# An attention and MoE kernel on one core: three VectorE operations in the weight conversion, new due times, and transposes in early gaps

## The chip, the cores and the metric

The kernel runs on one core of a Trainium2 chip. The metric is the device time of one execution in microseconds (us), the median of the runs shown. The engines are TensorE (PE, with weight loads listed apart as PEld), VectorE (DVE), ScalarE (ACT), GpSimd (POOL) and SyncE (SP, which here only issues DMAs). Each engine works through its own queue in order; they wait for each other through semaphores.

## What is computed

A linear attention over 8 batches, 8 heads, 576 positions and 64 columns feeds a two-layer network with a squared rectifier. The inputs lie in DRAM as 32-bit floats, apart from the two weight matrices, which are 64-bit floats; the output is 32-bit.

```
q_s = softmax of q over the columns of a head
k_s = softmax of k over the positions
kv  = k_s^T v                 per batch and head
x   = q_s kv                  laid out as 4608 tokens x 512
h   = x @ w_in                512 -> 2048
g   = s * max(h, 0)^2 + b
out = g @ w_out               2048 -> 512
```

## The kernel before

Matmuls run on fp32r values. To keep precision each weight, each `x` and each `g` is split into a high and a low part, and each product is three matmuls (high x high, high x low, low x high), 128 x 128 by 128 x 512.

The 4608 tokens are nine blocks: eight of 512 tokens, one for each batch (positions 0 to 511), and a last one made of the 64 positions left over of each batch. The hidden width of 2048 is cut into 16 pieces of 128, so a block has 16 steps. A step `t` (function `step`) is: 12 matmuls `h<-x,w` (line 975), then the rectifier on ACT (`r`, line 1000), squaring, scale and bias, the split into `gh` and `gl`, and 12 matmuls into `acc` (line 1038). In the even steps of the first block and in all later ones the middle goes DVE (line 1013), ACT (1015), DVE (1017). In the odd steps of the first block it goes ACT (1004), ACT (1006), ACT (1008), DVE (1010).

**Weights.** Weights arrive in 16 chunks `f` of 1 MB: `w_in` and `w_out` parts of one hidden piece, fetched on SP's queue by `load_w` into a staging tile `st`, where the low word `lo` and the high word `hi` of each 64-bit weight lie side by side. `conv_w` turns a chunk into 32-bit floats with integer and float operations on the two words, and splits it. Before the change it does this, each line one instruction on 1024 elements a partition (chunk 0 in two halves):

- ACT, line 204: `low` = `lo` scaled by 2^-29, as an integer
- ACT, line 207: `lo` = absolute value of `hi`, as floats
- DVE, line 210: the two top bits of `low` = those of `hi`, its sign among them
- DVE, line 215: clamp `lo` between C_MIN and C_MAX
- DVE, line 217: mask `lo` and shift it left by 3
- DVE, line 220: `low` = `lo` + `low`; from here the staging tile is free for a later chunk
- ACT, line 225: `w` high = `low` rounded to fp32r
- DVE, line 227: `w` low = `low` - `w` high

Chunk `f` is needed by step `f` of the first block (its `w_in` half by `h`, its `w_out` half by `acc`). So all 16 conversions stand beside the first block, as does the attention of batch 1. The attention of batch 0 stands before it. That attention is, for a pair of heads `u`, `k_stream` (maximum, `early` = exp, transposes, copies), `kv_stream` (`kv` matmuls and the blocks `kvf`), and `q_stream` (maximum, subtraction, exp, sum, division, transpose `qT`, copy to `early` in line 437, matmuls `xp` in line 444, cast to `x` in line 450, low part in line 453). The first step can end only when all four `x` of batch 0 are there.

**What sets the order.** Each piece of work is a generator that yields `Op`s: engine, an assumed cost, a due time, what it needs, which buffers it takes and frees. `Order.run` walks a model of the engines: among the operations of one engine that could start within 0.1 us of the earliest, it takes the one with the lowest due time, and then emits its instructions. The order on every queue, SP's and POOL's among them, is fixed by that when the program is built. Due times are in steps: `DUE_K`, `DUE_Q` and `DUE_V` have an entry for each pair of heads (batch 0 first, then batch 1) or each group of two pairs, and a conversion of chunk `f` is due at `f - AHEAD`, the first at `DUE_W`. A due time orders only operations that compete; it delays nothing by itself.

**Gaps on PE.** When the model sees PE without work for some time, it calls `idle`, which issues transposes of the identity into a PSUM bank that is not in use yet (`unused`, the bank tagged `h`), 60% of the gap at 0.109 us each. This ends when the first step takes the bank.

**Buffers.** PSUM: `acc` two, `big`, `sm` and `h` one each. SBUF: three `tmp` (the `low` of a conversion takes one), 17 `w` (staging tiles and finished weights).

Of the kernel before, what the change touches and what calls it, by code (L numbers as in the profile page):

```python
# [8 lines left out]
F32 = mybir.dt.float32  # L9
F32R = mybir.dt.float32r  # L10
I32 = mybir.dt.int32
U32 = mybir.dt.uint32
U16 = mybir.dt.uint16
AF = mybir.ActivationFunctionType
ALU = mybir.AluOpType
AX = mybir.AxisListType


C_MIN = 2.0 ** -15
C_MAX = float.fromhex("0x1.dffffep+16")  # L20

# [3 lines left out]
def attention_moe(ctx: ExitStack, tc: tile.TileContext, q, k, v, w_in, w_out, s, b, out):  # L27
    nc = tc.nc
# [3 lines left out]
    P = 128  # L32
# [5 lines left out]
    TB = NQ * P  # L38
    NTMP = 3
    NFE = 5  # L40
    AHEAD = 1
    PACE = 6

    DUE_K = (-42.5, 0, -33.5, -16, 6.5, 14, 12.5, 8.5)
    DUE_Q = (-8.5, -4.5, -2, -1, 13.5, 9.5, -29, 88.5)
    DUE_V = (-80, -87.5, -7.5, 14)
    DUE_W = -8
    assert DM == H * D and DM == NP * P and 2 * D == P and 2 * LEFT == P and B * LEFT == TB

    const = ctx.enter_context(tc.tile_pool(name="const", bufs=1))  # L50
# [6 lines left out]
    ps = ctx.enter_context(tc.tile_pool(name="ps", bufs=1, space=bass.MemoryType.PSUM))  # L57


    ident = const.tile([P, P], F32, name="ident")  # L60
# [57 lines left out]
    class Order:  # L118
# [28 lines left out]
        def run(self, streams):  # L147
            heads = [[next(g), 0.0, g] for g in streams]
            while heads:
                can = [(self.start(o, ready), i) for i, (o, ready, g) in enumerate(heads)]  # L150
                can = [(t, i) for t, i in can if t is not None]
                first, i = min(can)
                eng = heads[i][0].eng
                t, i = min(
                    ((t, i) for t, i in can if heads[i][0].eng == eng and t <= first + self.NEAR),
                    key=lambda c: (heads[c[1]][0].due, c),
                )
                o, ready, g = heads[i]
                if eng == "PE":

                    self.idle(t - self.at[eng], "h" in o.take)

                heads[i][1] = end = self.at[eng] = t + o.cost * (2 if eng == "PE" and t < self.COLD else 1)
                if o.kb:
                    self.pipe = max(self.pipe, end) + o.kb / 1024 / self.RATE
                    end = self.pipe + self.TRIP
                for tag in o.take:
                    self.taken[tag] += 1
                for tag in o.free:
                    self.freed[tag].append(end + self.HOP)  # L170
                for n in o.gives:
                    self.done[n] = end, "DMA" if o.kb else eng
                heads[i][0] = after = next(g, None)
                if after is None:
                    del heads[i]
                elif not o.kb and (eng != "PE" or after.eng != eng):
                    heads[i][1] = end + self.HOP
# [14 lines left out]

    def conv_w(f, some):

        due = f - AHEAD if f else DUE_W
        n = some.stop - some.start
        two = n / 2
        last = some.stop == 2
        yield Op("ACT", 1.04 * two, due, needs=[f"w{f} {i} there" for i in range(some.start, some.stop)], take=["tmp"])
        stg = wst[f][:, some]  # L200
        lo, hi = stg[:, :, :, 0], stg[:, :, :, 1]
        low = work.tile([P, n, DO], U32, name=f"low{some.start}_{f}", tag="tmp", bufs=NTMP)

        nc.scalar.activation(low.bitcast(I32), lo, AF.Copy, scale=2.0 ** -29)
        yield Op("ACT", 1.04 * two, due)

        nc.scalar.activation(lo.bitcast(F32), hi.bitcast(F32), AF.Abs)  # L207
        yield Op("DVE", 0.6 * two, due)

        nc.vector.tensor_scalar(  # L210
            low.bitcast(U16).rearrange("p n (e t) -> p n e t", t=2)[:, :, :, 1], stg.bitcast(U16)[:, :, :, 3],
            0xC000, None, op0=ALU.bitwise_and
        )
        yield Op("DVE", 0.6 * two, due)
        nc.vector.tensor_scalar(lo.bitcast(F32), lo.bitcast(F32), C_MIN, C_MAX, op0=ALU.max, op1=ALU.min)
        yield Op("DVE", 0.6 * two, due)
        nc.vector.tensor_scalar(lo, lo, 0x07FFFFFF, 3, op0=ALU.bitwise_and, op1=ALU.logical_shift_left)
        yield Op("DVE", 1.13 * two, due, free=["w"] if last else (), gives=[f"w{f} {some.stop} read"])

        nc.vector.tensor_tensor(out=low, in0=lo, in1=low, op=ALU.add)  # L220
        yield Op("ACT", 0.98 * two, due, take=["w"] if some.start == 0 else ())
        if not wt[f]:
            wt[f] = wpool.tile([P, 2, 2, DO], F32R, name=f"w_{f}", tag="w")
        w = wt[f][:, some]
        nc.scalar.copy(w[:, :, 0], low.bitcast(F32))
        yield Op("DVE", 1.13 * two, due, free=["tmp"], gives=[f"w{f} {i}" for i in range(some.start, some.stop)])
        nc.vector.tensor_tensor(out=w[:, :, 1], in0=low.bitcast(F32), in1=w[:, :, 0].bitcast(F32), op=ALU.subtract)
        for i in range(n):
            if some.start + i == 0:
                wi[f] = w[:, i].rearrange("p t (c e) -> p t c e", c=NP)  # L230
            else:
                wo[f] = w[:, i]
# [93 lines left out]
    def k_stream(u):  # L326
        pr, i = divmod(u, 2)
        due, (tag, bufs) = DUE_K[u], wide(u)
        yield Op("PE", 0.6, due, needs=[f"k{u} there"], take=["big", "ke"])
# [22 lines left out]
    def k_pair(pr):  # L352
        us = (2 * pr, 2 * pr + 1)
        due = DUE_K[us[0]]

# [24 lines left out]
    def kv_second(pr):  # L380
        due = DUE_V[pr]
        yield Op("PE", 1.4, due, needs=[f"k{u}" for u in (2 * pr, 2 * pr + 1)] + [f"v{pr} there"], take=["sm"], gives=[f"kv{pr}"])
# [8 lines left out]
    def kv_stream(pr):  # L391
        us = (2 * pr, 2 * pr + 1)
        due = DUE_V[pr]
        yield Op("DVE", 0.33, due, needs=[f"z{u}" for u in us])
# [9 lines left out]
    def q_stream(u):  # L404
        pr, i = divmod(u, 2)
        bb, hp = divmod(u, NP)
        due, (tag, bufs) = DUE_Q[u], wide(u)

# [125 lines left out]
    def begin(pr):  # L534

        bb, hq = divmod(pr, NP // 2)
        return NFC * bb + PACE * hq

# [448 lines left out]
    def step(t):  # L987

        blk, f = divmod(t, NFC)
        first = blk == 0  # L990
        parts = h_parts(t)
        for c in range(NP):
            yield Op(
                "PE", 0.68, t - 1, needs=[f"x{blk * NP + c}"] + ([f"w{t} 0"] if first else [f"o{t - 2} {NQ - 1}"]), take=["h"] if c == 0 else (),
                gives=[f"h{t}"] if c == NP - 1 else ()
            )
            hp_ = next(parts)
        yield Op("ACT", 0.5, t - 2, take=["r", "g"], free=["h"])
        r, gh, gl = g_tiles(t)
        nc.scalar.activation(r, hp_, AF.Relu)  # L1000
        if first and (t % 2):

            yield Op("ACT", 0.67, t - 2)
            nc.scalar.activation(r, r, AF.Square)
            yield Op("ACT", 0.75, t - 2)
            nc.scalar.activation(r, r, AF.Identity, bias=b_col, scale=s_col)
            yield Op("ACT", 0.51, t - 2)
            nc.scalar.copy(gh, r)  # L1008
            yield Op("DVE", 0.6, t - 2, free=["r"], gives=[f"g{t}"])
            nc.vector.tensor_tensor(out=gl, in0=r, in1=gh.bitcast(F32), op=ALU.subtract)  # L1010
        else:
            yield Op("DVE", 0.66, t - 2)
            nc.vector.scalar_tensor_tensor(out=r, in0=r, scalar=s_col, in1=r, op0=ALU.mult, op1=ALU.mult)  # L1013
            yield Op("ACT", 0.62, t - 2)
            nc.scalar.activation(gh, r, AF.Identity, bias=b_col)  # L1015
            yield Op("DVE", 0.66, t - 2, free=["r"], gives=[f"g{t}"])
            nc.vector.scalar_tensor_tensor(  # L1017
                out=gl, in0=r, scalar=b_col, in1=gh.bitcast(F32), op0=ALU.add, op1=ALU.subtract
            )
        parts = o_parts(t)  # L1020
        for i, j in enumerate(range(NQ)):
            yield Op(
                "PE", 0.68, t + 0.5, needs=[f"w{t} 1"] * first + [f"o{t - 1} {j}"] * (t > 0),
                take=["acc"] if f == 0 and j % 2 == 0 else (), free=["g"] if i == NQ - 1 else (), gives=[f"o{t} {j}"]
            )
            next(parts)
# [96 lines left out]
    def reload(pr):  # L1123

        p = 0 if pr == NP // 2 else pr - 1
        due = DUE_K[2 * pr] - 2

# [26 lines left out]
    tiles.update({pr: raws[pr % 2 if pr < 2 else 0] for pr in range(NU // 2)})  # L1154
    unused = [ps.tile([P, 512], F32, name="unused", tag="h")]

    def idle(us, last):
        if last:
            unused.clear()
        for _ in range(int(0.6 * us / 0.109) if unused else 0):  # L1160
            nc.tensor.transpose(unused[0][:, 0:P], ident, ident)

    order = Order({
        "acc": 2, "big": 1, "sm": 1, "h": 1, "r": 1, "g": 2, "ke": 1, "qf": 1, "qe": 2, "m2": 1, "m1": 1, "top": 1,
# [48 lines left out]
```

## Time and profile before

| | us |
|---|---|
| median of 3 runs (864.58 to 866.68) | 864.78 |
| the profiled execution | 866.32 |
| its span, first to last instruction | 864.4 |
| ScalarE busy | 440.2 |
| GpSimd busy | 167.2 |
| first run of twelve `h` matmuls without a pause between begins at | 38.5 |
| first block's last `h` run begins at | 131.77 |

How to read the profile's lines: times are from the start of the span. In a line of the order of time, the first number is the start, the second the length, and what stands in brackets is the engine's idle time before it and what released it. In a group, the numbers behind the bar are busy time in us and the mean of one in ns, and behind the next bar idle time before them and what ended it. A tile's name stands for all its buffers: `low`, `st`, `w` are those of all chunks. The profiled execution was one of the slower of the runs; the median of the runs is 1.54 us below it.

### The profile page before, as it was taken

How to read it: one execution, taken by the hardware profiler on the slowest of the kernel's cores; microseconds unless marked ns; L12 is line 12 of the kernel's file. 1: busy time of each engine (PE TensorE's matmuls, PEld its weight loads, DVE VectorE, ACT ScalarE, POOL GpSimd, SP SyncE). 2: the span in 40 equal slices, each digit the busy share in tenths (PEclk: the TensorE clock that was granted, in tenths of full speed). 3: DMA queues.
4: the chain of work that ended last, by engine and by line, in shares of the span. 5: the costliest groups of instructions: out<-in, count | busy, mean ns of one | idle time of the engine just before them, and what ended most of it. 6: DMA issues, size and time to landing. Idle time of an engine off the chain costs nothing.

```text
span 864.4 us, 11736 instructions
## 1 busy us (share of the span) xinstructions
PE 846.2 (98%) x4319; PEld 696.1 (81%) x4319; DVE 613.1 (71%) x949; ACT 440.2 (51%) x741; POOL 167.2 (19%) x184
## 2 busy tenths in 40 slices
PE   7799999999999999999999999999999999999997
PEld 6578887888888888888888888888888878888886
DVE  6999997696868687877586857695667686756400
ACT  5988955454554445444444444454436455555300
POOL 1000001120202020202020202120114446881000
PEclk9999999999999999999999999999999999999999
DMA  9994216515252434333424214421430110000100
GB/s 220 274 367 171 56 41 150 140 40 132 91 133 64 107 89 132 89 83 89 128 71 105 85 69 94 127 61 56 122 89 3 50 50 1 1 0 1 50 25 24
DMA packets 109992, 79.45 MB, mean 92 GB/s; under 512 B 60656, under 2 KB 103664, under 8 KB 109808
## 3 DMA queue, kind: packets, MB, share of 16 engines
q1 hardware_dynamic: 108496, 77.60, 32.2%
q10 hardware_dynamic: 1440, 1.12, 0.4%
q8 instruction: 34, 0.56, 0.3%
q14 instruction: 22, 0.18, 0.1%
HBM read 60.29 MB, written 18.40 MB: 91 GB/s over the span
## 4 chain that ended last, share of the span: by engine, by line
PE 90%; DVE 3%; ACT 2%; issue 1%; DMA 1%; SPq 1%; ACTq 0%
PE acc L1038 39%; PE h L975 34%; PE q L865 7%; PE last L961 5%; PE kv L303 2%; PE qa L865 1%; PE xp L680 1%; PE xq L680 1%; DMA area<-in_k_dram 1%; DMA raw<-in_k_dram 1%; PE xp L444 0%; ACT st L207 0%; SPq L276 0%; DVE w L935 0%; SPq L283 0%
## 5 line engine op out<-in xcount | busy, mean ns | idle before, releaser
L975 PE MATMUL h<-x,w 128*128 128x512 f32 x1344 | 329.7, 393 | 2.2 <-ACT r L1000 1.2
L1038 PE MATMUL acc<-w,gh 128*128 128x512 f32 x1024 | 319.1, 393 | 0.9 <-ACT gh L1008 0.9
L975 PEld LDWEIGHTS h<-x,w 128*128 128x128 f32 x1344 | 252.2, 189 | 56.9 <-ACT r L1000 1.9
L1038 PEld LDWEIGHTS acc<-w,gh 128*128 128x128 f32 x1024 | 190.6, 188 | 40.5 <-ACT gh L1008 1.3
L1038 PE MATMUL acc<-w,gl 128*128 128x512 f32 x512 | 200.3, 391 | 0.9 <-DVE gl L1010 0.6
L1000 ACT ACTIVATE r<-h 128x512 f32<-128x512 f32 x112 | 66.9, 597 | 176.0 <-PE h L975 170.5
L1013 DVE SCALAR_TENSOR_TENSOR r<-r,sb 128x512 f32<-128x512 f32 x104 | 83.6, 804 | 89.7 <-ACT r L1000 89.2
L1038 PEld LDWEIGHTS acc<-w,gl 128*128 128x128 f32 x512 | 96.4, 188 | 22.0 <-DVE gl L1010 1.1
L1015 ACT ACTIVATE gh<-r,sb 128x512 fp32r<-128x512 f32 x104 | 75.3, 724 | 61.6 <-DVE r L1013 61.1
L1017 DVE SCALAR_TENSOR_TENSOR gl<-r,sb,gh 128x512 fp32r<-128x512 f32 x104 | 80.6, 775 | 32.0 <-ACT gh L1015 30.6
L579 POOL TENSOR_TENSOR area<-area,qm 128x640 f32<-128x640 f32 x24 | 33.1, 1382 | 162.8 <-DVE qm L577 162.7
L596 POOL TENSOR_TENSOR qe<-qe,qr 128x640 f32<-128x640 f32 x24 | 32.5, 1358 | 65.2 <-DVE qr L592 46.4
L961 PE MATMUL last<-w 128*128 128x512 f32 x192 | 43.7, 389 | 0.0
L961 PEld LDWEIGHTS last<-w 128*128 128x128 f32 x192 | 36.0, 188 | 7.5
L660 POOL TENSOR_TENSOR spare<-kvf,spare 128x256 fp32r<-128x256 f32 x12 | 10.1, 844 | 118.6 <-issue 112.8
L935 DVE SCALAR_TENSOR_TENSOR gl<-r,sb,gh 128x512 fp32r<-128x512 f32 x16 | 16.2, 1014 | 16.8 <-ACT gh L933 16.8
L686 ACT COPY y<-xp 64x320 f32<-64x320 f32 x48 | 20.2, 420 | 13.5 <-PE xp L680 13.1
L690 DVE TENSOR_TENSOR y<-xp,y 64x320 f32<-64x320 f32 x48 | 23.5, 489 | 3.0 <-ACT y L686 2.0
L566 ACT ACTIVATE area<-area 128x640 f32<-128x640 f32 x24 | 17.7, 737 | 15.1 <-DVE area L528 13.3
L568 POOL MEMSET area<- 64x128 f32 x24 | 4.8, 200 | 101.5 <-issue 74.5
L600 DVE STREAM_TRANSPOSE area<-qe 128x640 f32<-128x640 f32 x24 | 19.9, 830 | 5.2 <-POOL qe L596 5.2
L1064 ACT COPY last<-last 128x512 f32<-128x512 f32 x3 | 1.8, 587 | 42.7 <-PE last L961 42.7
(184 smaller groups left out, 1094.2 us busy)
## 6 DMA issues: line engine op xcount, KB each, us to landing
st<-in_moe_w_in_dram SPq DMA_DIRECT2D x16, 512.0 KB, 8.5
st<-in_moe_w_out_dram SPq DMA_DIRECT2D x16, 512.0 KB, 9.0
out_dram<-o SPq DMA_DIRECT2D x16, 512.0 KB, 2.6
turned<-area SPq DMA_DIRECT2D x24, 320.0 KB, 2.3
qT<-turned SPq DMA_DIRECT2D x48, 160.0 KB, 3.0
area<-in_k_dram SPq DMA_DIRECT2D x14, 512.0 KB, 4.2
area<-in_q_dram SPq DMA_DIRECT2D x14, 512.0 KB, 5.5
area<-in_v_dram SPq DMA_DIRECT2D x56, 128.0 KB, 4.8
```

Source lines behind the costliest of these rows:

```text
L579: nc.gpsimd.tensor_tensor(out=qt, in0=qt, in1=bc(qm, [P, 2, NT, D]), op=ALU.subtract)
L596: nc.gpsimd.tensor_tensor(out=qe_, in0=qe_, in1=qr, op=ALU.mult)
L686: nc.scalar.copy(y[half[h], at], parts[h][a][half[1 - h]])
L690: nc.vector.tensor_tensor(out=y[half[h], at], in0=parts[h][a][half[h]], in1=y[half[h], at], op=ALU.add)
L865: nc.tensor.matmul(BANK[where], w(a)[:, c * P:(c + 1) * P], xs[b_][:, c], start=k in (0, 1, 3) and n == 0, stop=n == 5, skip_group_check=True)
L961: nc.tensor.matmul(t_, g[:, js], w_, start=(f == 0 and i == 0), stop=(f == NFC - 1 and i == 2))
L975: nc.tensor.matmul(hp_, w[:, j, c, :], x[:, c, :], start=(c == 0 and i == 0), stop=(c == NP - 1 and i == 2))
L1000: nc.scalar.activation(r, hp_, AF.Relu)
L1013: nc.vector.scalar_tensor_tensor(out=r, in0=r, scalar=s_col, in1=r, op0=ALU.mult, op1=ALU.mult)
L1015: nc.scalar.activation(gh, r, AF.Identity, bias=b_col)
L1017: nc.vector.scalar_tensor_tensor(out=gl, in0=r, scalar=b_col, in1=gh.bitcast(F32), op0=ALU.add, op1=ALU.subtract)
L1038: nc.tensor.matmul(acc[blk, j // 2][:, j % 2], g[:, js], w_, start=(f == 0 and i == 0), stop=(f == NFC - 1 and i == 2))
```

## The change

Five things are changed.

- **The conversion.** Masks are gone. The high word is clamped first on DVE, to both sides. ACT then applies a parametric rectifier: scaled by 2^-112 for positive weights, and for negative ones by -(2^32) more, so that the result is positive for both and its exponent is 32 higher for the negative. That difference is one bit, which the shift by 3 brings into the place of the sign. The shift and the joining with `low` are one DVE instruction (`scalar_tensor_tensor`, shift and or). `low` is scaled by 0.936 x 2^-29, so that it is at most 7 and stays within the three bits that the shift leaves free.
- **Due times.** Each chunk has its own (`DUE_C`), and those of keys, queries and values of the first two batches are other numbers.
- **Steps.** In the first block a step takes the ACT form where `ON_ACT` is positive, which is step 1 alone, and no longer in every odd step.
- **Gaps on PE.** After `unused` is over and up to 45 us of the model's time, gaps are filled with transposes into the `sm` bank, if nothing uses it then.
- `C_MIN` is no longer needed; `C_MAX` has the same value.

```diff
-    AHEAD = 1
+    DUE_C = (-24.0, -23.0, -2.0, -1.5, 8.5, -22.0, 14.5, 4.0, 7.5, 8.5, 5.0, 12.5, 46.0, 80.0, 63.5, 91.0)
+    ON_ACT = (-18.0, 41.5, -75.0, -103.0, -28.5, -54.0, -81.5, -151.5, -112.0, -141.5, -97.5, -151.5, -168.0, -217.0, -102.0, -87.5)
     PACE = 6
+    WARM = 45
...
-    DUE_K = (-42.5, 0, -33.5, -16, 6.5, 14, 12.5, 8.5)
-    DUE_Q = (-8.5, -4.5, -2, -1, 13.5, 9.5, -29, 88.5)
-    DUE_V = (-80, -87.5, -7.5, 14)
-    DUE_W = -8
+    DUE_K = (-100.5, 25.0, -40.5, -58.5, 6.0, -32.0, 12.5, 22.0)
+    DUE_Q = (-99.5, 69.5, -50.0, -13.0, 14.5, 13.5, -74.0, 34.5)
+    DUE_V = (-170.5, -122.0, -119.0, 9.0)
...
-                    self.idle(t - self.at[eng], "h" in o.take)
+                    free = self.freed["sm"]
+                    self.idle(t - self.at[eng], "h" in o.take, self.at[eng], len(free) == self.taken["sm"] and max(free, default=0) < self.at[eng])
...
-        due = f - AHEAD if f else DUE_W
+        due = DUE_C[f]
...
-        nc.scalar.activation(low.bitcast(I32), lo, AF.Copy, scale=2.0 ** -29)
+        nc.scalar.activation(low.bitcast(I32), lo, AF.Copy, scale=0.936 * 2.0 ** -29)
+        yield Op("DVE", 0.6 * two, due)
+
+        hi = hi.bitcast(F32)
+        nc.vector.tensor_scalar(hi, hi, C_MAX, -C_MAX, op0=ALU.min, op1=ALU.max)
         yield Op("ACT", 1.04 * two, due)
...
-        nc.scalar.activation(lo.bitcast(F32), hi.bitcast(F32), AF.Abs)
-        yield Op("DVE", 0.6 * two, due)
-
-        nc.vector.tensor_scalar(
-            low.bitcast(U16).rearrange("p n (e t) -> p n e t", t=2)[:, :, :, 1], stg.bitcast(U16)[:, :, :, 3],
-            0xC000, None, op0=ALU.bitwise_and
-        )
-        yield Op("DVE", 0.6 * two, due)
-        nc.vector.tensor_scalar(lo.bitcast(F32), lo.bitcast(F32), C_MIN, C_MAX, op0=ALU.max, op1=ALU.min)
-        yield Op("DVE", 0.6 * two, due)
-        nc.vector.tensor_scalar(lo, lo, 0x07FFFFFF, 3, op0=ALU.bitwise_and, op1=ALU.logical_shift_left)
+        nc.scalar.activation(lo.bitcast(F32), hi, AF.Prelu, scale=2.0 ** -112, alpha=-(2.0 ** 32))
         yield Op("DVE", 1.13 * two, due, free=["w"] if last else (), gives=[f"w{f} {some.stop} read"])
...
-        nc.vector.tensor_tensor(out=low, in0=lo, in1=low, op=ALU.add)
+        nc.vector.scalar_tensor_tensor(out=low, in0=lo, scalar=3, in1=low, op0=ALU.logical_shift_left, op1=ALU.bitwise_or)
...
-        if first and (t % 2):
+        if first and ON_ACT[t] > 0:
...
-    def idle(us, last):
+    def idle(us, last, at, sm):
         if last:
             unused.clear()
-        for _ in range(int(0.6 * us / 0.109) if unused else 0):
-            nc.tensor.transpose(unused[0][:, 0:P], ident, ident)
+        n = int(0.6 * us / 0.109)
+        if unused:
+            t = unused[0]
+        elif sm and n and at < WARM:
+            t = ps.tile([P, 512], F32, name=f"fill_{int(100 * at)}", tag="sm", bufs=1)
+        else:
+            n = 0
+        for _ in range(n):
+            nc.tensor.transpose(t[:, 0:P], ident, ident)
```

More of the change, by code (lines that the diff above doesn't have):

```diff
@@ L16 @@
 AX = mybir.AxisListType
-C_MIN = 2.0 ** -15
-C_MAX = float.fromhex("0x1.dffffep+16")
+C_MAX = float.fromhex("0x1.dffffep16")
 @with_exitstack
```

## The prediction

> **What bounds the kernel now.** I read the page's first part and the waits of TensorE, then TensorE's order of time for the first 70 us, then the table of windows around the places where it was slow, then the groups of instructions of the first 140 us with shapes kept apart, and last ScalarE's order of time in the few microseconds in front of the first long matmul run.
>
> ```profile
> span 864.4 us, 11736 instructions
> ...
> PE 846.2 (98%) x4319; PEld 696.1 (81%) x4319; DVE 613.1 (71%) x949; ACT 440.2 (51%) x741; POOL 167.2 (19%) x184
> ```
>
> TensorE (PE) is busy 98% of the span, so the change can only win back time in which PE stands or runs slowly. In the waits, PE's pauses after 66 us are three, the longest being:
>
> ```profile
> PE q L865 <- ACT r L914: 1.2, 1, 1.2
> ```
>
> That lies far behind the changed code. What is left to win lies before 70 us. The windows show it (length, then busy time and instruction count of PE, PEld, DVE, ACT, POOL, granted clock, DMA share, GB/s):
>
> ```profile
> 26.00:38.50 12.50, 8.12 (x57) 5.17 (x53) 10.90 (x17) 12.44 (x22) 0.00 (x0) 1.00 1.09 323
> 38.50:43.00 4.50, 4.50 (x13) 3.54 (x14) 4.50 (x7) 3.71 (x4) 0.00 (x0) 0.62 0.32 54
> ...
> 59.40:68.60 9.20, 7.70 (x26) 5.84 (x26) 9.17 (x13) 7.51 (x9) 0.00 (x0) 0.81 1.06 378
> 68.60:132.00 63.40, 63.40 (x357) 51.98 (x357) 61.73 (x89) 50.83 (x75) 1.23 (x8) 1.00 0.28 78
> ```
>
> Read them so. Up to 38.5 us PE works 8.12 of 12.5 us and ScalarE (ACT) is full, 12.44 of 12.5: the start waits for ACT. From 38.5 PE runs, at first with a granted clock of 0.62. At 59.4 to 68.6 it stands 1.5 us and has a clock of 0.81. From 68.6 to 132 VectorE (DVE) is 97% busy and yet PE never stands: DVE relief in that stretch is worth nothing by itself, and matters only because PE, if it comes earlier, asks for its weights earlier.
>
> ```profile
> 38.50 4.61 PE L975 MATMUL h<-x,w 128*128 128x512 f32 x12 [1.01 <-ACT r L1000]
> ...
> 60.31 0.73 PE L1038 MATMUL acc<-w,gh 128*128 128x512 f32 x2 [0.86 <-ACT gh L1008]
> 61.68 0.50 PE L1038 MATMUL acc<-w,gl 128*128 128x512 f32 x1 [0.64 <-DVE gl L1010]
> ```
>
> A run of twelve such matmuls at full rate has this length in the chain that ended last:
>
> ```profile
> 68.60 2.72 PE acc L1038 x12
> ```
>
> So the run at 38.50 lost 4.61 - 2.72 = 1.9 us to the clock. The stretch 59.4 to 68.6 holds one run of acc and one of h, 5.44 us at full rate, and took 9.20: 3.8 us lost, started by ACT's `gh` (L1008) and DVE's `gl` (L1010), the end of a step whose rectifying goes through four ACT instructions.
>
> **The conversion of a chunk.** The groups of 0 to 140 us, DVE's first, then ACT's (shapes, count, busy us, mean ns, idle before):
>
> ```profile
> L227 DVE TENSOR_TENSOR w<-low,w 128x1024 fp32r<-128x1024 f32 x15 | 18.3, 1218 | 1.1 <-ACT w L225 1.1
> L220 DVE CUSTOM_DVE_ANT_0 low<-st,low 128x2048 uint16<-128x2048 uint16 x15 | 18.2, 1216 | 0.0
> L210 DVE TENSOR_SCALAR low<-st 128x1024 uint16<-128x1024 uint16 x15 | 11.1, 760 | 0.0
> L217 DVE TENSOR_SCALAR st<-st 128x1024 uint32<-128x1024 uint32 x15 | 10.3, 689 | 0.0
> L215 DVE TENSOR_SCALAR st<-st 128x1024 f32<-128x1024 f32 x15 | 10.2, 687 | 0.1
> ...
> L1013 DVE SCALAR_TENSOR_TENSOR r<-r,sb 128x512 f32<-128x512 f32 x8 | 6.0, 745 | 0.5 <-ACT r L1000 0.5
> L1017 DVE SCALAR_TENSOR_TENSOR gl<-r,sb,gh 128x512 fp32r<-128x512 f32 x8 | 5.9, 744 | 0.1
> ...
> L1010 DVE TENSOR_TENSOR gl<-r,gh 128x512 fp32r<-128x512 f32 x8 | 5.5, 685 | 2.7 <-ACT gh L1008 2.7
> ```
>
> ```profile
> L207 ACT ACTIVATE st<-st 128x1024 f32<-128x1024 f32 x15 | 17.6, 1173 | 0.1
> ...
> L1006 ACT ACTIVATE r<-r,sb 128x512 f32<-128x512 f32 x8 | 6.5, 816 | 0.2
> L1015 ACT ACTIVATE gh<-r,sb 128x512 fp32r<-128x512 f32 x8 | 5.8, 724 | 0.8 <-DVE r L1013 0.8
> ...
> L1004 ACT ACTIVATE r<-r 128x512 f32<-128x512 f32 x8 | 5.1, 638 | 0.2
> L1008 ACT CAST gh<-r 128x512 fp32r<-128x512 f32 x8 | 4.9, 618 | 0.2
> ```
>
> Removed on DVE: L210, L215, L217 and L220, 0.760 + 0.687 + 0.689 + 1.216 = 3.35 us a chunk. Added: a clamp with the shape and stride of L215, 0.69 us, and one scalar_tensor_tensor on 1024 elements. That one isn't in the trace. L1013 and L1017 take 60 ns more than the plain L1010 at the same 512 elements, so from L220 I take 1.25 us; the ends are 1.22 us (as L220) and 2.43 us (twice L220, should shift and or on words run as slowly as two passes). A chunk then costs DVE 1.41 us less, and 15 whole chunks with the two halves of the first make 16: 22.6 us less. On ACT, Prelu takes the place of Abs with the same shape; I take 1.17 us (L207); a table load beside it is a rival (below). The chain of a chunk now changes engine five times instead of three.
>
> **The steps of the first block.** Only step 1 keeps the ACT form, so seven odd steps change. Each gives ACT 0.638 + 0.816 + 0.618 - 0.724 = 1.35 us back, 9.4 in all, and costs DVE 0.745 + 0.744 - 0.685 = 0.80 us, 5.6 in all. DVE's net is 22.6 - 5.6 = 17.0 us less. Its load to 132 us was 97% full, so PE could not have come 5 us earlier without this; with it, it can, and at the worst end of the new instruction (16 x 1.18 us more, 18.9) that cover is just gone.
>
> **The start.** The planner's due times move too. In front of 38.5 us ACT's row and PE's row read:
>
> ```profile
> 29.95 1.24 PE L444 MATMUL xp<-early,kvf 128*128 128x256 f32 x4 [0.76 <-ACT early L437]
> 31.03 0.71 PE L434 MATMUL qT<-ident,qe 128*128 128x128 f32 x5
> 33.35 1.24 PE L444 MATMUL xp<-early,kvf 128*128 128x256 f32 x4 [1.61 <-ACT early L437]
> ...
> 36.76 0.73 PE L975 MATMUL h<-x,w 128*128 128x512 f32 x2 [0.34 <-DVE x L453]
> ```
>
> ```profile
> 31.01 1.18 ACT L204 ACTIVATE low<-st 128x1024 int32<-128x1024 uint32 x1
> 32.08 0.58 ACT L450 CAST x<-xp 128x512 fp32r<-128x512 f32 x1
> ...
> 32.64 0.65 ACT L437 COPY early<-qT 128x576 f32<-128x576 f32 x1
> 33.17 1.19 ACT L207 ACTIVATE st<-st 128x1024 f32<-128x1024 f32 x1
> 34.22 1.19 ACT L204 ACTIVATE low<-st 128x1024 int32<-128x1024 uint32 x1
> 35.26 0.61 ACT L450 CAST x<-xp 128x512 fp32r<-128x512 f32 x1
> ...
> 36.78 1.19 ACT L207 ACTIVATE st<-st 128x1024 f32<-128x1024 f32 x1
> 37.83 0.62 ACT L1000 ACTIVATE r<-h 128x512 f32<-128x512 f32 x1
> ```
>
> The last head's way to the first step waits three times behind conversions of later chunks: the copy of `qT` (ready 31.74, begun 32.64: 0.90), the cast of `x` (34.59, 35.26: 0.67) and the rectifier (37.49, 37.83: 0.34), 1.9 us together. Of the new dues of batch 0's keys and queries, six of eight lie ahead of those of chunks 2 to 4 (-2, -1.5, 8.5), so these conversions should now stand behind. I take 1.7 us earlier. The ends are 0.5 us later (chunk 5, at -22, and the first head's query, at 69.5, are put where they can hurt; what stands behind a late instruction on ACT is the next head) and 3.5 us earlier (the 1.9 and PE's two waits of 0.76 and 1.61 for `early`, in part the same time).
>
> The dues move issues on SP's queue as well: reloads of batch 1 and the fetches of chunks 5 on stand there in planned order, and the query reload waits for both heads. DMA moved only 54 GB/s in 38.5 to 43, so I cost that at nothing; if a fetch came over 5 us later, the chunk would miss its step.
>
> **The fillers.** PE's planned gaps up to 45 us are filled to 60% with transposes, now also after the first step began.
>
> ```profile
> 2.46 4.53 PE L1161 MATMUL unused<-ident 128*128 128x128 f32 x20 [2.46 <-POOL ident masks.py:199]
> ...
> 12.21 1.69 PE L1161 MATMUL unused<-ident 128*128 128x128 f32 x14
> ```
>
> Here a filler took 4.53 / 20 = 0.23 us at first and 1.69 / 14 = 0.12 us at 12 us, with hardly anything but transposes between: they do bring PE to its fast pace. So of the 1.9 us after 38.5 I take 1.4 (ends 0 and 1.9). A filler that stands where PE no longer waits costs its 0.12 us.
>
> The Trainium skill, page "TensorE: Matmul & The Clock Gate", section "Part 4: PE-mode transpose", speaks against this: it says that transposes don't count as busy time for the clock in the same way, and that the full clock doesn't engage in them. By it the 1.4 would be 0 and the whole gain 4.1 us; the two rows above speak against the page.
>
> **Sum.** Start 1.7, clock 1.4, the stretch at 59.4: 3.3 of 3.8 (its step goes over DVE's shorter way, but its matmuls still need weights in time), less 0.9 for small new pauses, since the whole order is planned anew (ends 0 and 3). That is 5.5 us. Against the profiled execution, 866.32 us (span 864.4 and 1.9 around it), it gives 860.8. The median of the runs shown, 864.78, is 1.5 below that execution; from it: **859.3 us**.
>
> **Rivals.**
> (1) The start doesn't move, since the attention chain and not the conversions set it: 1.4 + 3.3 - 0.9 = 3.8 us, 861.0. For it speaks that the longer chain of a chunk delays chunk 1, which is itself needed near 38 us.
> (2) The pause of 59.4 is replaced by one like it: five engine changes a chunk, each behind an instruction of up to 1.2 us, or a dear scalar_tensor_tensor, make a chunk late, and PE cools again. Then 1.7 + 1.4 - 0.9 = 2.2 us, 862.6: within 0.3%, which is about what a measurement of this kernel can tell from no change. Against it: 17 us less on DVE and 9.4 less on ACT.
> (3) Slower: Prelu is not in the table that Exp uses, and each change between them loads one.
>
> ```profile
> L1115 ACT ACT_TABLE_LOAD x1 | 1.3, 1283 | 5.4 <-DMA area<-in_q_dram 5.4
> ```
>
> One load served Exp, Copy, Abs, Relu, Square and Identity so far, which speaks against it. If it happens, I estimate three alternations of Exp and Prelu ahead of 38.5, where ACT is full: 6 x 1.28 = 7.7 us on the path. The gains without the start, 3.8, go against it: 3.9 slower, 868.7. From six loads on the path it outweighs the whole gain by more than 0.3%.
> The Trainium skill, page "ScalarE: Activation LUTs", section "Table sets: the hidden batching unit", has this rule: functions come in sets, cheap ones are in every set, and a change of set costs about 2.66 us with its drain. It doesn't list this rectifier; by its price the six loads would be 16 us.
>
> **Chances.** Forecast 0.55, (1) 0.20, (2) 0.17, (3) with other mishaps 0.08. All of the forecast and of (1) and a little of (2) are faster by over 0.3%: 0.79. Same 0.14, slower 0.07. The range: the best ends, 3.5 + 1.9 + 3.8 = 9.2, give 855.6, and a pause less later on one more; at the other side it takes in (1) and (2): 854.5 to 863.8.
>
> **What would show it.** Right: twelve h matmuls of step 1 begin near 36.8 us and take 2.7 to 3.2; no granted clock below 0.9 from 40 to 70; DVE's three conversion groups near 0.69, 1.25 and 1.22 us with DVE well under 97% from 68 to 125; one table load. Wrong: Prelu at more than 1.2 us, a second ACT_TABLE_LOAD, a scalar_tensor_tensor over 1.5 us, or a new wait of PE for `w`, `gl` or `gh` over 1 us in 40 to 130.

## The result and the profile after

| | before | after |
|---|---|---|
| median of 20 runs (us) | 864.68 | 866.19 |
| range (us) | 864.13 to 866.68 | 865.01 to 869.23 |
| span of the profiled execution (us) | 864.4 | 866.2 |

The ratio after/before is 1.0021, with a 95% interval of 1.0015 to 1.0027. The change is a small loss, about 1.5 us, where 859.3 us was forecast. The profile below is of an execution of 867.97 us, 1.78 above the median. Lines of the changed kernel's code have numbers 5 lower than before (`h` is L970, `xp` L439, `qT` L429).

The first part of the page after, with the busy time of each engine:

```profile
span 866.2 us, 11765 instructions
...
PE 848.4 (98%) x4347; PEld 698.7 (81%) x4347; DVE 600.1 (69%) x922; ACT 432.1 (50%) x727; POOL 170.0 (20%) x184
```

VectorE works 13.0 us less than before and ScalarE 8.1 us less, and the end is later all the same. The groups of the first 140 us of the changed kernel, shapes kept apart:

```profile
L215 DVE SCALAR_TENSOR_TENSOR low<-st,low 128x1024 uint32<-128x1024 uint32 x15 | 18.2, 1216 | 0.8 <-ACT st L212 0.8
...
L209 DVE TENSOR_SCALAR st<-st 128x1024 f32<-128x1024 f32 x15 | 10.3, 687 | 0.0
```

```profile
L212 ACT ACTIVATE st<-st 128x1024 f32<-128x1024 f32 x15 | 17.4, 1160 | 0.8 <-DVE st L209 0.7
...
L1110 ACT ACT_TABLE_LOAD x1 | 1.3, 1283 | 4.9 <-DMA area<-in_q_dram 4.9
```

So the new instructions cost what was forecast: the clamp 0.687 us, the shift and or 1.216, the rectifier 1.160, and one table load in all. TensorE's order of time around the start of the second block says where the time went:

```profile
118.64 0.77 PE L429 MATMUL qT<-ident,qe 128*128 128x128 f32 x5
...
136.71 0.71 PE L429 MATMUL qT<-ident,qe 128*128 128x128 f32 x5
138.20 1.24 PE L439 MATMUL xp<-early,kvf 128*128 128x256 f32 x4 [0.78 <-ACT early L432]
140.11 0.49 PE L970 MATMUL h<-x,w 128*128 128x512 f32 x1 [0.68 <-ACT x L445]
140.95 0.73 PE L970 MATMUL h<-x,w 128*128 128x512 f32 x2 [0.35 <-DVE x L448]
142.37 4.61 PE L970 MATMUL h<-x,w 128*128 128x512 f32 x12 [0.69 <-ACT r L995]
```

Step 16, the first of block 1, needs all four `x` of batch 1. The last head's transposes, its `xp`, the last quarter of step 16's `h` and the `h` of step 17 follow each other here with nothing to fill between: TensorE stands for 0.78, 0.68, 0.35 and 0.69 us, 2.5 together, and then runs twelve matmuls in 4.61 us.

### The profile page after: what moved, and what is told of

The parts are those of the page before. It is cut to its first block, busy times and chain, and to the rows that moved or that the text cites. A ratio compares the mean times of both kernels' runs of the same rounds, so it can differ in the third digit from the quotient of the medians.

```text
span 866.2 us, 11765 instructions
## 1 busy us (share of the span) xinstructions
PE 848.4 (98%) x4347; PEld 698.7 (81%) x4347; DVE 600.1 (69%) x922; ACT 432.1 (50%) x727; POOL 170.0 (20%) x184
## 4 chain that ended last, share of the span: by engine, by line
PE 88%; DVE 5%; ACT 3%; issue 2%; DMA 1%; SPq 0%; ACTq 0%; DVEq 0%
PE acc L1033 37%; PE h L970 33%; PE q L860 7%; PE last L956 5%; PE kv L298 2%; PE qa L860 1%; PE xp L675 1%; DVE w L222 1%; PE xp L439 1%; PE xq L675 1%; DMA area<-in_k_dram 1%; DVE st L209 1%; DMA st<-in_moe_w_in_dram 1%; DVE r L1008 1%; DVE low L215 0%
## 5 line engine op out<-in xcount | busy, mean ns | idle before, releaser
L970 PE MATMUL h<-x,w 128*128 128x512 f32 x1344 | 330.9, 393 | 2.6 <-ACT r L995 1.0
L970 PEld LDWEIGHTS h<-x,w 128*128 128x128 f32 x1344 | 251.5, 189 | 56.9 <-DVE x L448 2.1
L1008 DVE SCALAR_TENSOR_TENSOR r<-r,sb 128x512 f32<-128x512 f32 x111 | 87.1, 785 | 88.7 <-ACT r L995 88.4
L1012 DVE SCALAR_TENSOR_TENSOR gl<-r,sb,gh 128x512 fp32r<-128x512 f32 x111 | 89.1, 803 | 34.4 <-ACT gh L1010 33.2
L1010 ACT ACTIVATE gh<-r,sb 128x512 fp32r<-128x512 f32 x111 | 80.4, 724 | 62.0 <-DVE r L1008 61.5
L930 DVE SCALAR_TENSOR_TENSOR gl<-r,sb,gh 128x512 fp32r<-128x512 f32 x16 | 16.4, 1027 | 16.2 <-ACT gh L928 16.2
L298 PEld LDWEIGHTS kv<-area 128*64 128x64 f32 x600 | 19.3, 141 | 5.3 <-issue 4.9
```

The costliest lines, as they stand in the source:

```text
L298: nc.tensor.matmul(kv[h * D:(h + 1) * D, i], kt[:, i, h, n], vt[:, 2 * i + h, n], start=(n == 0), stop=(n == NT - 1))
L970: nc.tensor.matmul(hp_, w[:, j, c, :], x[:, c, :], start=(c == 0 and i == 0), stop=(c == NP - 1 and i == 2))
L1012: nc.vector.scalar_tensor_tensor(out=gl, in0=r, scalar=b_col, in1=gh.bitcast(F32), op0=ALU.add, op1=ALU.subtract)
```

## The experiments

**A second profile of both kernels.** The forecast was worked from one execution of the kernel before that took 866.32 us, 1.6 above the median. Both kernels were profiled once more, unchanged.

> The kernel before, unchanged, profiled a second time. Theory A (the 866.32 us of the profile that the prediction was worked from was a slow sample, and its cold stretches at 38.5 and 59.4 us are in part its own): a span near 862.5 us, the twelve h matmuls of step 1 in about 3.0 us instead of 4.61, and less than the 1.5 us of pause-and-clock loss kept at 59.4 to 68.6 (at a granted clock of 1.00 the stretch takes about 9.2 less 1.3). Theory B (those losses belong to every execution of the kernel before, so a cure for them must show in the median): a span near 864.4 us again, 4.6 us for step 1's h and a clock near 0.62 and 0.81 in the two stretches.

> The changed kernel, unchanged, profiled a second time. Theory A (the time goes at block 1 in every execution): a span of 863.5 to 866.2 us, step 1's h begins at 39.0 to 39.5 us (0.7 us less late than in its first profile, in which the start ran at a lower clock) but still later than the 38.24 us of the kernel before, and 2 to 2.5 us of TensorE's idle time at 132 to 150 us with the h of step 17 in about 4.6 us. Theory B (the boundary was a matter of that one execution): no more than 0.5 us of idle time at 132 to 150 us and step 17's h in 2.9 us.

The kernel before took 864.31 us (span 862.4), the changed one 865.56 (span 863.8). The windows of the kernel before, second execution (length, then busy time and count of PE, PEld, DVE, ACT, POOL, granted clock, DMA share, GB/s):

```profile
38.50:43.00 4.50, 4.50 (x21) 3.69 (x21) 4.50 (x7) 4.46 (x6) 0.00 (x0) 1.00 0.33 53
43.00:59.40 16.40, 15.15 (x65) 11.58 (x63) 15.43 (x21) 13.66 (x18) 0.00 (x0) 1.00 1.03 362
59.40:68.60 9.20, 7.96 (x34) 6.31 (x35) 9.17 (x13) 8.14 (x12) 0.00 (x0) 1.00 1.06 378
68.60:132.00 63.40, 63.40 (x358) 51.94 (x357) 62.86 (x92) 50.67 (x75) 1.43 (x8) 1.00 0.29 82
132.00:150.00 18.00, 17.80 (x80) 14.24 (x79) 12.70 (x22) 9.30 (x15) 4.33 (x4) 1.00 0.48 129
```

And of the changed kernel, second execution:

```profile
43.00:59.40 16.40, 16.13 (x71) 13.03 (x70) 14.84 (x21) 14.76 (x19) 0.00 (x0) 1.00 1.03 357
59.40:68.60 9.20, 9.20 (x42) 7.64 (x41) 9.20 (x11) 9.05 (x12) 0.00 (x0) 1.00 1.06 378
68.60:132.00 63.40, 63.32 (x356) 51.42 (x355) 52.45 (x77) 43.04 (x62) 1.17 (x7) 1.00 0.34 94
132.00:150.00 18.00, 15.51 (x66) 11.47 (x65) 13.96 (x22) 7.00 (x13) 5.27 (x4) 1.00 0.59 160
```

The cold stretches of the first profile, those with a granted clock well below 1 (0.62 and 0.81), are not there in the second one of the same kernel; its pause at 59.4 is, with 1.24 us. In the changed kernel that pause is gone, and at 132 to 150 TensorE stands 2.49 us where it stood 0.20. So the idle time at the boundary comes back, as theory A has it. The 4.61 us of step 17 that it expected do not: they are 3.02 here, at a clock of 1.00 in that window where the first profile has 0.91. TensorE's `h` runs, in order of time and without the `acc` rows between them, put numbers to it. Before, second execution:

```profile
38.24 3.01 PE L975 MATMUL h<-x,w 128*128 128x512 f32 x12 [1.00 <-ACT r L1000]
...
49.92 0.73 PE L975 MATMUL h<-x,w 128*128 128x512 f32 x2 [0.50 <-ACT w L225]
51.18 2.56 PE L975 MATMUL h<-x,w 128*128 128x512 f32 x10 [0.53 <-DVE w L227]
56.30 2.88 PE L975 MATMUL h<-x,w 128*128 128x512 f32 x12
63.76 2.88 PE L975 MATMUL h<-x,w 128*128 128x512 f32 x12
...
140.15 2.88 PE L975 MATMUL h<-x,w 128*128 128x512 f32 x12
```

After, second execution:

```profile
39.42 3.03 PE L970 MATMUL h<-x,w 128*128 128x512 f32 x12 [0.38 <-ACT r L995]
...
56.45 2.88 PE L970 MATMUL h<-x,w 128*128 128x512 f32 x12
61.89 2.88 PE L970 MATMUL h<-x,w 128*128 128x512 f32 x12
...
141.60 3.02 PE L970 MATMUL h<-x,w 128*128 128x512 f32 x12 [0.69 <-ACT r L995]
```

Steps 1, 4, 5 and 17 begin 1.18 us later, 0.15 later, 1.87 earlier and 1.45 later than before; the span ends 1.4 later. So the changed kernel starts late, wins 3.05 us between steps 1 and 5, and gives back 3.32 between steps 5 and 17. Of these 3.32 the idle time of the last two windows shows 2.29 + 0.08 = 2.37. The rest shows in the same rows when they are read from start to start. After, second execution, a head with work behind it and the last head:

```profile
121.23 1.13 PE L439 MATMUL xp<-early,kvf 128*128 128x256 f32 x4
121.96 2.48 PE L970 MATMUL h<-x,w 128*128 128x512 f32 x9
124.28 0.71 PE L429 MATMUL qT<-ident,qe 128*128 128x128 f32 x5
124.74 0.94 PE L970 MATMUL h<-x,w 128*128 128x512 f32 x3
...
135.93 0.71 PE L429 MATMUL qT<-ident,qe 128*128 128x128 f32 x5
```

Where other work follows at once, the next row begins 0.46 us after a `qT`, 0.73 after an `xp`, and three `h` matmuls take 0.68 of the 2.72 from one run of twelve to the next row: 1.87 together. The last head takes 5.67 for the same, from 135.93 to the `h` of step 17 at 141.60. That is 3.80 lost, more than the idle time, because a row's end overlaps the next row only where there is no pause. The kernel before loses 0.45 at its last head (`qT` at 132.43, next row at 133.34). The difference is 3.35, so the boundary accounts for the whole of the 3.32.

The first profile of the changed kernel, 2.4 us longer, begins step 17 0.77 later (0.64 of it already at step 1) and takes 4.61 for it (3.02 here).

**One due time moved.** If the last `x` of batch 1 are late because of their due times, one number should bring back most of the loss.

```diff
-    DUE_Q = (-99.5, 69.5, -50.0, -13.0, 14.5, 13.5, -74.0, 34.5)
+    DUE_Q = (-99.5, 69.5, -50.0, -13.0, 14.5, 13.5, -74.0, 4.0)
```

> Theory A (the microseconds won before 70 us are given back where block 1 begins, because the last x of batch 1 comes late there): with the eighth query due at 4 instead of 34.5, the four heads of batch 1 are spread, step 16 ends its h matmuls 2 to 5 us earlier than in the changed kernel (141.7 us), no matmul run there has a halved clock, and the whole kernel is 2 to 5 us faster than the changed one, 0.1 to 0.4% faster than the kernel before. Theory B (the loss is the later start, step 1 at 40.06 us instead of 38.50): nothing of that is touched, so the time stays within 0.5 us of the changed kernel. Theory C (the later blocks or the tail were ordered worse): also no change, and the place where step 16 ends doesn't show in the total.

Measured: 863.37 us, ratio to the kernel before 0.9986 (0.9977 to 0.9995), 2.8 us less than the changed kernel. Step 1 still begins at 39.36, so theory B falls. The window at the boundary, in this run:

```profile
132.00:150.00 18.00, 17.93 (x78) 14.15 (x77) 12.34 (x21) 7.01 (x12) 5.44 (x4) 1.00 0.61 164
```

The first and the last of TensorE's heads of batch 1 in this run, and its steps 5 and 17:

```profile
63.37 2.88 PE L970 MATMUL h<-x,w 128*128 128x512 f32 x12
...
95.50 0.71 PE L429 MATMUL qT<-ident,qe 128*128 128x128 f32 x5
...
101.87 1.14 PE L439 MATMUL xp<-early,kvf 128*128 128x256 f32 x4
...
130.40 0.71 PE L429 MATMUL qT<-ident,qe 128*128 128x128 f32 x5
...
132.34 1.13 PE L439 MATMUL xp<-early,kvf 128*128 128x256 f32 x4
...
139.45 2.88 PE L970 MATMUL h<-x,w 128*128 128x512 f32 x12
```

The four heads use one PSUM buffer in turn, `big`. In the changed kernel the first of the four begins only at 118.64, and the last `xp` is at 138.20; in this run one head goes at 95.50 and the last `xp` is at 132.34, while block 0 still has matmuls for TensorE. From step 5 to step 17 this run takes 76.08 us, the changed kernel 79.71 and the kernel before 76.39 (second profiles). The wait is gone, and with it the loss: the late last `x` of batch 1 is what made the changed kernel slower than the one before. (The profiled execution, 864.74 us, is the longest of the eleven; TensorE stands 1.48 us in it between 43 and 59.4, ahead of the stretch in question.)

**More due times.** The queries of batch 1 one after another, and a few chunks moved.

```diff
-    DUE_C = (-24.0, -23.0, -2.0, -1.5, 8.5, -22.0, 14.5, 4.0, 7.5, 8.5, 5.0, 12.5, 46.0, 80.0, 63.5, 91.0)
+    DUE_C = (-24.0, -23.0, -6.0, -1.5, 8.5, -22.0, 14.5, 4.0, 7.5, 0, 5.0, 12.5, 46.0, 80.0, 63.5, 91.0)
...
-    DUE_K = (-100.5, 25.0, -40.5, -58.5, 6.0, -32.0, 12.5, 22.0)
-    DUE_Q = (-99.5, 69.5, -50.0, -13.0, 14.5, 13.5, -74.0, 34.5)
-    DUE_V = (-170.5, -122.0, -119.0, 9.0)
+    DUE_K = (-100.5, 25.0, -40.5, -58.5, 6.0, -32.0, 10.5, 22.0)
+    DUE_Q = (-99.5, 69.5, -50.0, -12.0, 14.5, 9.5, 10.5, 2.0)
+    DUE_V = (-170.5, -122.0, 4.5, 9.0)
```

> The changed kernel with the queries of batch 1 due sooner one after another (9.5, 10.5 and 2.0 instead of 13.5, -74 and 34.5), and one value, one key head and three weight chunks moved a little. Theory A (the gain of the first 70 us is there, and is given back only because the last x of batch 1 are late for block 1): TensorE's waits at 132 to 150 us are gone as in the run with one due time moved, and the time is 861.0 to 863.2 us, 3 to 5 us less than the changed kernel. Theory B (an early loss that the due times can't reach): not under 864.5 us. Theory C (loss in later blocks): 866 us with the waits gone.

Measured: 863.00 us, ratio 0.9980 (0.9971 to 0.9989), span 861.1 in the profile. It is the lowest median of the study. Most of what it wins over the changed kernel is already in the one due time above.

**The conversion alone.** The kernel before with the new `conv_w` and nothing else, under the old due times.

```diff
-        due = DUE_C[f]
+        due = f - AHEAD if f else DUE_W
```

(The line taken out is that of the changed kernel; all else outside `conv_w` is as in the kernel before.)

> The kernel before with the new conversion alone: old due times, old odd steps, no new transposes. Theory A: VectorE has 22 us less to do and PE isn't short of weights, but the order is planned anew and nothing pulls the heads of batch 1 forward, so step 16 ends its h matmuls later than before (140.9 us) by 3 to 9 us and the kernel is slower than before by as much. Theory B (the conversion is a gain, the due times and the start are the loss): 3 to 5 us faster than before.

Measured: 874.25 us, ratio 1.0116 (1.0101 to 1.0132), 9.7 us slower with 34 VectorE instructions fewer (two for each of 15 chunks and two halves). Rows of its TensorE:

```profile
42.64 5.13 PE L969 MATMUL h<-x,w 128*128 128x512 f32 x12 [1.55 <-ACT r L994]
...
142.75 0.71 PE L428 MATMUL qT<-ident,qe 128*128 128x128 f32 x5
144.59 1.24 PE L438 MATMUL xp<-early,kvf 128*128 128x256 f32 x4 [1.14 <-ACT early L431]
...
148.76 3.02 PE L969 MATMUL h<-x,w 128*128 128x512 f32 x12 [0.69 <-ACT r L994]
```

Against the second profile of the kernel before, step 1 begins 4.4 us later and step 17 8.6 us later, behind the same late `xp`; the loss is a little more than the 3 to 9 us expected. The conversion in another order of engines makes another plan, and the old due times do not fit it. That it is the plan and not the instructions shows below, where the same conversion is run under old and new due times.

**The steps alone.** The kernel before with the seven later odd steps in the form of the even ones.

```diff
-        if first and (t % 2):
+        if first and t == 1:
```

> The kernel before with the seven later odd steps of block 0 in the form of the even ones; conversion, due times and fillers stay as before. Theory A (whatever comes earlier in block 0 is given back at block 1, as long as the due times of batch 1's heads are not made for it, since the order is planned anew and the last x then come late): the stretch at 59.4 us is passed sooner, by 1 to 3 us at the h of step 6, and yet the time is 3 to 8 us more than the kernel before, 868 to 873 us, with the last xp of batch 1 after 138 us and TensorE waiting for early, x and r behind it. Theory B (the step is a gain that stays): 861.3 to 863.3 us.

Measured: 872.15 us, ratio 1.0093 (1.0077 to 1.0108). Rows of its TensorE:

```profile
62.13 2.88 PE L975 MATMUL h<-x,w 128*128 128x512 f32 x12
...
143.48 1.13 PE L444 MATMUL xp<-early,kvf 128*128 128x256 f32 x4
145.29 0.50 PE L975 MATMUL h<-x,w 128*128 128x512 f32 x1 [0.67 <-ACT x L450]
```

Step 5 begins 1.6 us earlier than before (62.13 for 63.76), as step 5 and not step 6 takes the win; step 6 at 69.74 is already 0.5 later, so the expectation missed there. The last `xp` is again behind 138, at 143.48. Part of the loss arises earlier than at block 1: TensorE is busy only 60.63 of the 63.4 us from 68.6 to 132, the stretch in which VectorE is 63.13 busy:

```profile
68.60:132.00 63.40, 60.63 (x333) 46.90 (x333) 63.13 (x93) 44.36 (x63) 2.00 (x8) 1.00 0.30 84
```

TensorE's waits there end about half with VectorE (`gl`, `w`, `x`: 1.5 us) and half with ScalarE (`early`, `gh`: 1.3). VectorE was 62.86 us busy in this stretch before, so it had little room for these steps without the cheaper conversion; no run shows that apart from the new plan.

**All old due times.** The changed kernel with `DUE_C`, `DUE_K`, `DUE_Q` and `DUE_V` as they were before.

```diff
-    DUE_C = (-24.0, -23.0, -2.0, -1.5, 8.5, -22.0, 14.5, 4.0, 7.5, 8.5, 5.0, 12.5, 46.0, 80.0, 63.5, 91.0)
+    DUE_C = (-8,) + tuple(range(15))
...
-    DUE_Q = (-99.5, 69.5, -50.0, -13.0, 14.5, 13.5, -74.0, 34.5)
+    DUE_Q = (-8.5, -4.5, -2, -1, 13.5, 9.5, -29, 88.5)
```

(`DUE_K` and `DUE_V` likewise)

> The changed kernel with all the due times of the kernel before: the new conversion, the new steps of block 0 and the fillers stay. Theory A (the new conversion by itself moves everything in the order that is planned, and the new due times are what mends that, up to one value): slower than the changed kernel, 867 to 873 us, with chunk conversions ahead of the heads at the start and step 1's h beginning after 41 us. Theory B (the new due times themselves are the fault, the conversion and the steps are a gain): near 861 to 864 us, faster than the kernel before.

Measured: 872.22 us, ratio 1.0092 (1.0078 to 1.0106). Step 1's `h` begins at 40.77, just short of the 41 expected. The new due times are worth 6.0 us to the changed kernel, though one of them costs it 2.8.

**VectorE relieved, the order kept.** The kernel before without two instructions of every chunk; the plan keeps its entries for them.

```diff
-        nc.vector.tensor_scalar(
-            low.bitcast(U16).rearrange("p n (e t) -> p n e t", t=2)[:, :, :, 1], stg.bitcast(U16)[:, :, :, 3],
-            0xC000, None, op0=ALU.bitwise_and
-        )
...
-        nc.vector.tensor_scalar(lo.bitcast(F32), lo.bitcast(F32), C_MIN, C_MAX, op0=ALU.max, op1=ALU.min)
```

> The kernel before without two of VectorE's operations in every chunk (the and of the top bits, 0.76 us, and the clamp, 0.69 us); the weights then come out wrong, and the planned order stays as it is, instruction for instruction. VectorE has 1.45 us a chunk less, about what the change saves. Theory A (VectorE is hidden in the kernel before but for the wait of step 3 for its weights and the pause at 60 us, which belongs to gh and gl): 0 to 1.5 us less than the kernel before, so 863.1 to 864.6 us, with about 1 us of PE's idle time between 43 and 59.4 us gone. Theory B (VectorE's load to 132 us sets the pace): 2 to 5 us less, under 862.6 us.

Measured: 863.90 us, ratio 0.9993 (0.9984 to 1.0002): not told apart from no change. So 1.45 us a chunk, what the new conversion saves, is worth at most 1.4 us (0.0016 of 864.5) where nothing else moves. VectorE, busy as it was, held up the kernel before by no more than that.

**The fillers.** Three runs: the fillers alone on the kernel before, the changed kernel without them, and the same with the one due time moved.

```diff
-    WARM = 45
+    WARM = 0
```

> The kernel before with the transposes alone. Theory A: step 1 begins as before and takes 2.7 to 3.1 us instead of 4.61; of the 1.6 us at most 0.8 reach the end, since in the kernel before step 16 had only so much room at the last x of batch 1; total 0 to 0.8 us faster than before. Theory B: 1.6 us faster (0.19%).

> The changed kernel without the transposes after the first step began. Theory A: step 1 runs with a halved clock again and loses 1.6 us there, but PE waits for the last x of batch 1 at the start of block 1 anyway, so the total stays within 0.5 us of the changed kernel. Theory B (what is won or lost early goes to the end): 1.6 us slower than the changed kernel.

> The changed kernel with the last query of batch 1 due at 4.0 and without the new fillers. The run without fillers alone took the time of the changed kernel (866.2), which theory A lays to the wait at block 1, which absorbs what is won or lost ahead of it. Theory A: with that wait gone the fillers count: 0.5 to 1.9 us more than the run with the query at 4.0 (863.4), so 863.9 to 865.3 us, with a granted clock near 0.62 at step 1 in its profile. Theory B (fillers are worth nothing in a typical run, since its clock is mostly up without them): 863.0 to 863.8 us.

Measured: the fillers alone 864.64 us, ratio 1.0000 (0.9991 to 1.0009). The changed kernel without fillers 866.22, ratio 1.0024 (1.0013 to 1.0035); with them 866.19. With the due time moved and without fillers 863.34, ratio 0.9987 (0.9978 to 0.9995); with them 863.37. The last one was to tell whether the wait at block 1 had hidden their worth. The medians show no worth in either case; but the profiled execution of that last run had a clock of 1.00 at step 1 and not the 0.62 expected, so a cold start without that wait was not seen. And yet the fillers do something. The window of step 1 in the changed kernel without fillers:

```profile
38.50:43.00 4.50, 3.98 (x10) 3.12 (x11) 4.50 (x6) 3.18 (x4) 0.00 (x0) 0.62 0.26 47
```

Six profiled executions had the fillers there, each with a granted clock of 1.00 in this window. Seven had none, and four of these were cold: 0.62 (before), 0.62 (above), 0.68 (VectorE relieved) and 0.50 (the conversion alone). Why the time does not follow is in the two profiles of the kernel before. With the cold clock step 1's `h` takes 4.61 us, with the full one 3.01; step 4 begins at 56.57 and at 56.30, although step 1 itself began 0.26 apart. The 1.6 us won are lost again at step 3, which comes earlier and then waits 0.50 and 0.53 for its weights `w` (the rows at 49.92 and 51.18 above).

## Why the prediction was wrong

- **Prices of the instructions: right.** 0.687, 1.216 and 1.160 us measured for 0.69, 1.25 and 1.17 taken, and one table load, so rival (3)'s mechanism did not occur. VectorE's total fell by 13.0 us and not by the net 17.0, since neighbours overlap and a removed instruction saves less than its length: in the second profile before, L210 began at 34.29, ran 0.77, and L215 began at 34.94. The run with VectorE relieved shows it alone: 16 times 1.45 is 23.2 us, and VectorE's total fell from 613.1 to 595.0, by 18.1. That VectorE's relief by itself is worth next to nothing held (ratio 0.9993), and in the changed kernel it is 52.45 of 63.4 us busy where it was 62.86.
- **"I take 1.7 us earlier" at the start: wrong, with the wrong sign.** Step 1 began 1.18 us later. "These conversions should now stand behind" is the step that failed. A due time orders only what can start at the same time; while a head's copy is not ready, a conversion that is ready goes ahead and holds ScalarE for over a microsecond. ScalarE's order of time after, second execution:

```profile
30.95 1.05 ACT L220 CAST w<-low 128x1024 fp32r<-128x1024 f32 x1
31.91 1.18 ACT L205 ACTIVATE low<-st 128x1024 int32<-128x1024 uint32 x1
32.99 0.56 ACT L445 CAST x<-xp 128x512 fp32r<-128x512 f32 x1
33.46 0.21 ACT L240 COPY misc<-xp 128x64 f32<-128x64 f32 x1
33.56 0.65 ACT L432 COPY early<-qT 128x576 f32<-128x576 f32 x1
34.09 1.16 ACT L212 ACTIVATE st<-st 128x1024 f32<-128x1024 f32 x1
35.12 1.15 ACT L205 ACTIVATE low<-st 128x1024 int32<-128x1024 uint32 x1
36.15 0.59 ACT L445 CAST x<-xp 128x512 fp32r<-128x512 f32 x1
```

  Two conversions still stand in front of each `x`, as before, so the 1.7 us were not won. The 1.18 were lost ahead of these rows, in the order of the heads among themselves. The fourth exp of batch 0's keys begins at 24.46 and not at 21.21, behind two exps of queries that stood behind it before (21.65 and 23.11 now, 23.05 and 27.37 then). The last blocks `kvf` then begin at 29.25 and not at 28.02, and the copies and casts of the last two heads are each 1.1 to 1.3 us later than before. This is read from the rows; no run changes that order alone. The ends given, 0.5 later to 3.5 earlier, did not hold it.
- **"Of the 1.9 us after 38.5 I take 1.4": the clock came up as forecast, the term was 0.** The clock at 38.5 to 43 us was 1.00 in all six executions with fillers and in three of the seven without, and with fillers it stayed at 1.00 up to 68.6 us. That speaks against the rule of the Trainium skill, page "TensorE: Matmul & The Clock Gate", section "Part 4: PE-mode transpose", by which transposes don't count as busy time for the clock in the same way; thirteen executions are few. But the kernel before is not cold in every execution, and where it was, step 3's late weights hid it. The loss itself was 1.6 us and not 1.9, as the run of twelve takes 3.01 there with the full clock. The term was taken without following it to the next wait. That wait is where the change did win: step 3 no longer stands 1.03 us for its weights (second profiles), which is not in the sum.
- **"The stretch at 59.4: 3.3": the mechanism right, the size 2.0.** From step 4 to step 5 the kernel before took 7.46 us in its second profile and the changed one 5.44. The rest of the 3.3 was the clock of 0.81, which the first profile had and the second had not: 8.74 us from step 4 to step 5 in the first (56.57 to 65.31).
- **"From it: 859.3": wrong base.** Terms read in an execution of 866.32 us were taken off the median. The clock loss at 59.4, 1.3 us, is most of the 2.0 us by which this execution was longer than the second one; it was counted as a gain and, by starting at the median, taken off a second time. The one at 38.5 had cost nothing by step 4. From 866.32 the same sum gave 860.8, and without the two clock terms (1.4 and 1.3 of the 3.3) it would have been 5.5 - 1.4 - 1.3 = 2.8 us off the median: 862.0.
- **"Less 0.9 for small new pauses": far too small.** This is the step that decided the sign. The boundary of block 1 took 3.3 us, against 3.05 won between steps 1 and 5, and the start 1.18 more. The due times of batch 1 stood in the diff, and the four heads, one PSUM buffer and the need of step 16 for all four in the code; the prediction looked for what is late only up to 130 us. Rival (2) came nearest (a pause replaced by another), but sought the pause at a chunk's weights, and it is at the last `x`.

## What to carry to other kernels

When an order is planned from costs, a cheaper operation is a new plan: ask of every later deadline (here the last input of the next block) whether it still has work beside it when the stretch ahead gets shorter. Work out terms from a profile that lies at the median, or from two, and take off nothing that only the slower one shows. Before pricing a gain, follow it to the next wait: here 1.6 us of clock were gone two steps later at a weight that came when it came.

## What was not expected of the hardware

The granted clock differs between executions of one program at one place: 0.62 and 1.00 in 38.5 to 43 us of the kernel before, and 0.91 and 1.00 in 132 to 150 us of the changed one, where the order of instructions is the same. How busy TensorE was ahead of it does not tell which it will be: of the 12.5 us up to 38.5 it was busy 8.12 in the execution with 0.62 and 7.89 in that with 1.00, and among the other runs without fillers 9.66 stands before a clock of 0.50 (the conversion alone) and 8.67 before one of 1.00 (the steps alone). With the fillers in that stretch it was busy 10.17 to 11.00, and the clock was 1.00 in every execution seen. How near such a stretch lies to the point at which the clock falls, these runs do not say.
